# Attention block: pairing half of the second unit's maxima through key differences held in a slot of their own, and starting the half-run order at the third step

## The chip, the cores and the metric

One Trainium2 chip, and on it one core. The metric is the device time of one execution in microseconds (us); of several executions the median is given. A profile is one further execution, taken by the hardware profiler.

## What is computed

A transformer block on 2048 tokens of width 576, in float32: an adaLN modulation from a vector c, softmax attention with 32 heads of 18, and a gated feed-forward part of width 4608. The case is about the attention:

```python
q, k, v = split_heads(h @ wqkv)                  # h: layernorm(x) * (1 + ca) + sa
scores = einsum("bhqd,bhkd->bhqk", q, k) * 18 ** -0.5
p = softmax(scores)                              # over the 2048 keys
x = x + ga * (einsum("bhqk,bhkd->bhqd", p, v) @ wo)
x = x + gb * ((sigmoid(h2 @ w_gate) * (h2 @ w_up)) @ w_down)
```

The softmax subtracts the largest score of every row, so these maxima must be known before the exponentials of the row are taken.

## The kernel before

**Units and steps.** Attention runs over 32 units: a unit is two heads (h = 0, 1) and one half of the queries (1024). Unit u has 16 steps (kt = 0 to 15), one for each 128 keys; step number `step` is 16 u + kt. A step computes four score tiles s of 128 keys by 512 queries (PE, L1010), takes their exponentials p (ACT, L1014), and multiplies the values into them (PE, L584, `values()`). The values lag by two steps (`LAG = 2`).

**Maxima, run ahead.** The generator `maxima()` finds the row maxima of a unit long before its steps. Each call (a "turn") multiplies 128 queries by 512 keys into one PSUM bank (PE, L479) and takes the largest of every row (DVE, L485, `tensor_reduce`). A unit has 64 turns: 8 blocks `qt` of queries, by two heads, by four blocks `kc` of keys. Four turns go with a step. 88 turns have run before step 0 (the 64 of unit 0 and the blocks qt = 0, 1, 2 of unit 1), so the turns of step n are 88 + 4n to 91 + 4n; unit 1's blocks qt = 4 to 7 are the turns of steps 2 to 9, and unit 2 begins at step 10. After a unit, L497 takes the maximum over kc, and `spread()` (a PE transpose, L510, and four DMAs, L519) writes it as two more rows of the q tile, where L1010 subtracts it.

**Pairs.** From unit 2 on (`SINGLE = (0, 1)` are the two left out), head 0 treats the key blocks 0 and 1 as a pair. The product for kc = 0 uses the differences of the keys of block 0 and block 1 in place of the keys of block 0; ACT applies Relu to it into the tile `over` (L488), and one DVE instruction (L490, `tensor_tensor_reduce`) adds the product of kc = 1 and takes the maximum, since max(a, b) = max(a - b, 0) + b. So of eight turns six are reduced by L485, one by L490 and one goes to ACT. Cell kc = 1 of the result is then not written, and a memset (L464, POOL) fills it with a low number. The differences are made during the projections (`key_differences`, POOL, L325 to L330), are written to the DRAM tile `kd` behind the keys, and come to the chip as columns 2048 to 2559 of a unit's key tile. The key tiles of units 0 and 1 (`t0`, `t1`) have 2048 columns and hold none.

**Two orders.** The instructions of PE and ACT are issued in the order in which the text writes them (`manual_schedule`). A pair of steps (even kt, odd kt) has one of two orders, written as letters: m a maxima turn, t a score tile with its exponential, v the values of one step, a and b its two halves, w, s, c, k side work. The plain order is "vtmmttmvtm", "ktmwttmctmm"; the order with half runs is "vmmtmmtsactt", "wmcmbkttmtmt". `state["halved"]` selects the second one; its condition has `step >= 10`, the step at which the pairs begin. It also sets the order of the eight turns (`MAXIMA_H`).

**Queues and space.** The order of DVE, POOL and SP (the queue that issues most DMAs) is set by a planner. An engine runs its instructions in order, so one that waits holds back those behind it. Between the projections and attention, `right.close()` frees the projection's pools on the right side: `hT` (the operand), `wpool` (weights) and `stage` (the tiles `pl`, from which L310 stores q and k to DRAM). In their space stand the pools `opool`, `big` and `slots`; `slots` has the key tiles k0, k1, k2 (units 2, 3, 4 and so on), whose rows of ones are set by a POOL memset (L425) ahead of the loads of `load_heads` (L447, L451), and two tiles w0 and w1 for background work. The first user of w0 is `load_mod` at step 16 in the text, a load of 288 KB (L101); with it go two loads of 1152 KB into `big` (L100). They are for `weigh`, a POOL chain (L114, L117), which `modulate` uses at step 34.

Of the kernel before, what the change touches and what calls it, by code (L numbers as in the profile page):

```python
# [15 lines left out]
F32 = mybir.dt.float32  # L16
F32R = mybir.dt.float32r
# [6 lines left out]
P = 128  # L24
S = 2048
# [3 lines left out]
DH = 18  # L29
VW = DH + 1  # L30
NT = S // P
NCH = S // 512
# [3 lines left out]
LOWEST = -3.4e38  # L36
# [10 lines left out]
LAG = 2  # L47

MAXIMA = ((1, 0), (0, 0), (1, 1), (0, 2), (1, 2), (0, 3), (0, 1), (1, 3))
SINGLE = (0, 1)  # L50
# [11 lines left out]
def tile_block(ctx, tc, x_in, wqkv, wo, w_gate, w_up, w_down, c_in, w_mod, out):  # L62
    nc = tc.nc
# [25 lines left out]
    def bank():  # L89

        turns["bank"] += 1
        return ps[turns["bank"] % 7].tile([P, 512], F32, name=f"s{turns['bank'] % 7}")
# [171 lines left out]
    kd = dram.tile([2, D, S + 512], F32R, name="kd")  # L264
# [165 lines left out]
    def heads(u):  # L430
        return qsets[u % 3], ksets[u if u < 2 else 2 + (u - 2) % 3]

    def load_heads(u):


        qs, ks = heads(u)
        half, p = divmod(u, H // 2)
        n = S if u < 2 else S + 512
        own = slice(half * HW, (half + 1) * HW)
        for h in range(2):  # L440
            rows = slice((2 * p + h) * DH, (2 * p + h + 1) * DH)
            two, one = (slice(64 * h + a, 64 * h + b) for a, b in ((0, 2 * DH), (2 * DH, 3 * DH)))
            nc.sync.dma_start(
                qs[two, :].bitcast(F32), qd[:, rows, own].rearrange("l f n -> f l n").bitcast(F32)
            )
            nc.sync.dma_start(qs[one, :].bitcast(F32), qd[0, rows, own].bitcast(F32))
            nc.sync.dma_start(  # L447
                ks[two, 0:n].bitcast(F32),
                kd[0, rows, 0:n].unsqueeze(1).to_broadcast([DH, 2, n]).bitcast(F32),
            )  # L450
            nc.sync.dma_start(ks[one, 0:n].bitcast(F32), kd[1, rows, 0:n].bitcast(F32))  # L451
# [3 lines left out]
    def maxima():  # L455


        n = HW // P
        last = None
        for u in range(UNITS):  # L460
            qs, ks = heads(u)
            mx = mxs[u % 2]
            if u not in SINGLE and u - 2 in SINGLE:
                nc.gpsimd.memset(mx[:, 0:n, 1], LOWEST)  # L464
            for i in range(8 * n):
                if last is not None and i == (9 if u == 1 else 8):
                    if u == 1:
                        for _ in spread(*last):
                            pass
                    else:  # L470
                        state["spread"] = last
                qt = i // 8
                pairs = u not in SINGLE
                h, kc = (MAXIMA_H if state.get("halved") else MAXIMA)[i % 8]
                rows = slice(64 * h, 64 * h + 3 * DH)
                paired = pairs and h == 0 and kc < 2
                at = NCH if paired and kc == 0 else kc
                sp = bank()
                nc.tensor.matmul(  # L479
                    sp, qs[rows, qt * P : (qt + 1) * P],  # L480
                    ks[rows, at * 512 : (at + 1) * 512], start=True, stop=True,
                )
                to = mx[:, h * n + qt, kc : kc + 1]
                if not paired:
                    nc.vector.tensor_reduce(to, sp, axis=AX.X, op=ALU.max)  # L485
                elif kc == 0:
                    over = small.tile([P, 512], F32, name="over", bufs=1)
                    nc.scalar.activation(over, sp, AF.Relu)  # L488
                else:
                    nc.vector.tensor_tensor_reduce(  # L490
                        out=over, in0=sp, in1=over, scale=1.0, scalar=LOWEST,
                        op0=ALU.add, op1=ALU.max, accum_out=mx[:, h * n + qt, 0:1],
                    )
                if i < 8 * n - 1:
                    yield
            nm = small.tile([P, 2, n], F32, name="nm")
            nc.vector.tensor_reduce(  # L497
                nm.rearrange("p h t -> p (h t)"), mx, axis=AX.X, op=ALU.max, negate=True
            )
            last = (qs, nm)  # L500
            yield
        for _ in range(8):
            yield
        state["spread"] = last

    def spread(qs, nm):

        n = HW // P
        tp = bank()[0 : 2 * n, 0:P]
        nc.tensor.transpose(tp, nm.rearrange("p h t -> p (h t)"), ident)  # L510
        yield
        mrows = small.tile([32 + 2 * n, P], F32R, name="mrows", bufs=1)
        parts = [mrows[32 * l : 32 * l + 2 * n] for l in range(2)]
        nc.scalar.copy(parts[0], tp)
        nc.vector.tensor_sub(parts[1], tp, parts[0].bitcast(F32))
        for h in range(2):
            for l, part in enumerate(parts):
                to = 64 * h + 3 * DH + l
                nc.sync.dma_start(  # L519
                    qs[to : to + 1, :].rearrange("l (t q) -> l t q", q=P).bitcast(F32),  # L520
                    part[n * h : n * (h + 1), :].bitcast(F32),
                )

    todo = maxima()
    state = {}

# [10 lines left out]
    with tc.tile_pool(name="wv1", bufs=1) as wvp:  # L537
# [3 lines left out]
        for i, parts in enumerate(tiles):  # L541
# [5 lines left out]
            for g in range(2):  # L547
                pl = project_qk([(wt, 2 * g), (wt, 2 * g + 1)], run if i else None)
                col, n = parts[-1]
# [11 lines left out]
    slots = ctx.enter_context(tc.tile_pool(name="slots", bufs=1, side="right"))  # L561
# [7 lines left out]
    bgs = ExitStack()  # L569
    bgp = bgs.enter_context(tc.tile_pool(name="bgp", bufs=1))  # L570
    load_heads(2)

    pending = []

# [390 lines left out]
    for u in range(UNITS):  # L965
        half, p = divmod(u, H // 2)
        qs, ks = heads(u)
# [4 lines left out]
        for kt in range(NT):  # L972
            step = u * NT + kt
            turns["to"] = 64 + 4 * LEAD + 4 * (step + 1)
            kcols = slice(kt * P, (kt + 1) * P)
            if kt % 2 == 0:
                heavy = state.get("next") == "g"
                hold = heavy and (kt == 2 or kt == 12 and u < UNITS - 1)
                state["halved"] = step >= 10 and (hold or not heavy)
            halved = state["halved"]  # L980
            sides = iter(SIDES_H if halved else SIDES)
            probs = [None] * 4
# [1 line left out]
            for does in order[kt % 2]:  # L984
# [21 lines left out]
                else:  # L1006
                    c, h = next(sides)
                    sT = bank()
                    rows = slice(64 * h, 64 * h + 3 * DH + 2)
# [6 lines left out]
            if u in (1, 3):  # L1016
                if kt == 0:
                    a = big.tile([P, 8, 640], F32, name="big")
                    a = a.rearrange("p a b -> p (a b)")[:, 0 : 8 * D].rearrange("p (t c) -> p t c", t=4)
                    b = slots.tile([P, 2560], F32, name="w0")[:, 0 : 2 * D]  # L1020
# [519 lines left out]
    for n, (hf, b, k) in enumerate(seq):  # L1540
# [6 lines left out]
        at = n % 7  # L1547
# [196 lines left out]
```

## Time and profile before

| what | value |
|---|---|
| time, median of 3 runs (lowest to highest) | 2807.12 us (2804.7 to 2808.96) |
| the profiled execution | 2804.28 us |
| its span, first to last instruction | 2802.5 us |
| PE busy | 2766.7 us, 99% |
| DVE busy | 2299.2 us, 82% |
| ACT busy | 1606.0 us, 57% |
| POOL busy | 818.1 us, 29% |
| DMA traffic | 462.60 MB, mean 165 GB/s |
| granted TensorE clock | 1.000 |

A busy share is an average over stages that differ. The attention begins at about 236 us of the span; what a change there is worth is read from that stretch of the trace. In rows of the timeline the first number is the start in us, the second the time from the first to the end of the last instruction of the row, and the bracket at the end is the engine's idle time before it with what ended it. In rows of the windows the columns are the stretch, its length, the busy time and (number) of PE, PEld, DVE, ACT and POOL, the granted clock, the DMA engines' share and GB/s.

### The profile page before, as it was taken

Reading aid. Unit: us, or ns where it says so; the run is one execution under the profiler, and the core shown is the slowest. Engines: PE = TensorE matmul, PEld = TensorE weight load, DVE = VectorE, ACT = ScalarE, POOL = GpSimd, SP = SyncE. Lnnn points to the kernel's source line nnn. Section 1 sums busy time; section 2 is a strip of 40 time slices with the busy share of each in tenths; the row PEclk is TensorE's granted clock in tenths of the full one; section 3 lists DMA queues with packets and bytes.
Section 4 is the critical chain, followed back from the end, with each engine's and each line's share of the span. In section 5 each row is a group of like instructions: output and inputs, shape, how many; then the busy total and the mean of one; then the engine's idle time right before and its main releaser. Section 6 shows DMA issues by size and latency. Waiting matters only on the chain.

```text
span 2802.5 us, 50859 instructions
## 1 busy us (share of the span) xinstructions
PE 2766.7 (99%) x18637; PEld 1832.7 (65%) x18637; DVE 2299.2 (82%) x4370; ACT 1606.0 (57%) x3051; POOL 818.1 (29%) x1077
## 2 busy tenths in 40 slices
PE   7999999999999999999999999999999999999999
PEld 5975444444444444444443888888888888888888
DVE  7278999999998888999883788888898677777777
ACT  3216999999999778999888322333333222222221
POOL 3125208887843111563103222222221100000000
PEclk9999999999999999999999999999999999999999
DMA  5344215444432120222126766667767966666663
GB/s 173 126 148 148 75 59 172 164 171 161 172 135 80 36 58 24 98 106 66 48 68 216 269 217 228 233 216 266 279 249 275 356 200 196 203 195 201 200 196 120
DMA packets 170778, 462.60 MB, mean 165 GB/s; under 512 B 21212, under 2 KB 88032, under 8 KB 160416
## 3 DMA queue, kind: packets, MB, share of 16 engines
q1 hardware_dynamic: 150064, 360.72, 38.5%
q0 software_dynamic: 20464, 98.62, 10.0%
q8 instruction: 147, 2.41, 0.4%
q14 instruction: 103, 0.84, 0.1%
HBM read 281.92 MB, written 176.82 MB: 164 GB/s over the span
## 4 chain that ended last, share of the span: by engine, by line
PE 94%; DVE 3%; DMA 1%; ACT 1%; issue 1%; SPq 0%; POOL 0%; ACTq 0%; DVEq 0%; POOLq 0%
PE x L1151 27%; PE o L584 19%; PE s L1010 12%; PE s L479 11%; PE d L1301 8%; PE d L1233 6%; PE s L298 4%; PE s L731 2%; PE s L349 2%; DVE mx L485 1%; PE s L611 1%; ACT p L1014 1%; DMA wm<-in_w_mod_dram 0%; PE d L1480 0%; DVE w L1141 0%
## 5 line engine op out<-in xcount | busy, mean ns | idle before, releaser
L1014 ACT ACTIVATE p<-s 128x512 f32<-128x512 f32 x2048 | 1078.3, 622 | 99.2 <-PE s L1010 86.0
L485 DVE TENSOR_REDUCE mx<-s 128x1 f32<-128x512 f32 x1568 | 994.9, 684 | 111.4 <-PE s L479 97.3
L584 PE MATMUL o<-p,vaug 128*32 128x256 f32 (+1 forms) x5848 | 592.4, 477 | 3.0 <-ACT p L1014 2.5
L1010 PE MATMUL s<-q,k 56*128 56x512 f32 x1920 | 516.7, 449 | 0.0
L479 PE MATMUL s<-k,q 54*128 54x512 f32 x1920 | 501.2, 427 | 2.6 <-DVE t L701 1.7
L479 PEld LDWEIGHTS s<-k,q 54*128 54x128 f32 x1920 | 275.7, 185 | 232.1 <-DVE mx L490 161.0
L1010 PEld LDWEIGHTS s<-q,k 56*128 56x128 f32 x1920 | 246.9, 184 | 242.4 <-issue 112.8
L1151 PE MATMUL x<-k,w 128*128 128x512 f32 x1512 | 368.7, 391 | 0.0
L1151 PEld LDWEIGHTS x<-k,w 128*128 128x128 f32 x1512 | 277.0, 188 | 53.2 <-issue 1.7
L1301 PE MATMUL d<-wd,hh 128*128 128x288 f32 x1248 | 249.9, 295 | 2.4 <-DVE Oa L1305 2.4
L584 PEld LDWEIGHTS o<-p,vaug 128*32 128x32 f32 x5848 | 115.3, 108 | 209.4 <-issue 130.7
L1151 PE MATMUL x<-big,w 128*128 128x512 f32 x1008 | 244.7, 391 | 1.4 <-DVE u L1645 0.7
L1151 PE MATMUL x<-w,w 128*128 128x512 f32 x1008 | 245.1, 391 | 0.0
L1151 PEld LDWEIGHTS x<-big,w 128*128 128x128 f32 x1008 | 185.2, 188 | 37.4 <-DVE u L1645 1.1
L1151 PEld LDWEIGHTS x<-w,w 128*128 128x128 f32 x1008 | 184.3, 188 | 34.4
L1301 PEld LDWEIGHTS d<-wd,hh 128*128 128x128 f32 x1248 | 202.1, 188 | 6.3 <-DVE Oa L1305 3.1
L1301 PE MATMUL d<-wd,hl 128*128 128x288 f32 x624 | 184.3, 295 | 0.0
L1305 DVE TENSOR_TENSOR Oa<-Oa,d 128x288 f32<-128x288 f32 x312 | 136.5, 453 | 54.6 <-PE d L1301 50.5
L490 DVE CUSTOM_DVE_ANT_0 over<-s,over 128x512 f32<-128x512 f32 x240 | 164.7, 686 | 0.8 <-ACT p L1014 0.3
L488 ACT ACTIVATE over<-s 128x512 f32<-128x512 f32 x240 | 150.3, 626 | 7.5 <-PE s L479 7.3
L1160 ACT ACTIVATE sg<-x 128x512 f32<-128x512 f32 x36 | 21.6, 599 | 207.4 <-PE x L1151 207.4
L1132 ACT CAST w<-S 128x768 fp32r<-128x768 f32 x71 | 59.3, 836 | 137.2 <-POOL S L1105 135.4
(274 smaller groups left out, 3894.2 us busy)
## 6 DMA issues: line engine op xcount, KB each, us to landing
ws<-w SPq DMA_DIRECT2D x126, 640.0 KB
w<-ws SPq DMA_DIRECT2D x126, 640.0 KB
wd<-wds SPq DMA_DIRECT2D x19, 1152.0 KB
k<-kd SPq DMA_DIRECT2D x60, 360.0 KB
wds<-w POOLq DMA_DIRECT2D x18, 1152.0 KB, 4.9
wtd<-t POOLq DMA_DIRECT2D x32, 576.0 KB, 4.7
wt<-wtd SPq DMA_DIRECT2D x64, 288.0 KB
wd<-wds SPq DMA_DIRECT2D x52, 288.0 KB
```

The costliest lines, as they stand in the source:

```text
L298: nc.tensor.matmul(acc, w, hT[:, t, cols], start=n == 0, stop=n == len(ts_) - 1)
L479: nc.tensor.matmul(sp, qs[rows, qt * P : (qt + 1) * P], ks[rows, at * 512 : (at + 1) * 512], start=True, stop=True,)
L485: nc.vector.tensor_reduce(to, sp, axis=AX.X, op=ALU.max)
L488: nc.scalar.activation(over, sp, AF.Relu)
L490: nc.vector.tensor_tensor_reduce(out=over, in0=sp, in1=over, scale=1.0, scalar=LOWEST, op0=ALU.add, op1=ALU.max, accum_out=mx[:, h * n + q ...
L584: nc.tensor.matmul(acc[32 * j : 32 * j + 32, cols], vaug[:, kt, (2 * p + h) * VW : (2 * p + h) * VW + 32], probs[2 * c + h][:, cols], star ...
L1010: nc.tensor.matmul(sT, ks[rows, kcols], qs[rows, c * 512 : (c + 1) * 512], start=True, stop=True)
L1014: state["exp"] = nc.scalar.activation(pr, sT, AF.Exp, scale=SCALE)
L1151: nc.tensor.matmul(acc[v], w[:, v, a, :], X[s][:, b, :], start=first and n == 0, stop=n == 6, skip_group_check=not first,)
L1233: nc.tensor.matmul(acc, a[:, rows], w[:, k, :], start=n == 0, stop=n == 2)
L1301: nc.tensor.matmul(acc[:, :HALF], a[:, f, rows], w[:, f, cols], start=n == 0, stop=n == 5)
L1305: nc.vector.tensor_add(Oa[:, t, cols], Oa[:, t, cols], acc[:, :HALF])
```

## The change

Unit 1's blocks qt = 4 to 7 are paired too. Their differences come from a new tile, `state["differences"]`: the first 512 columns of w0, loaded by four DMAs on SP right after `load_heads(2)`; both heads are loaded, in the row layout of a key tile. POOL sets the cells kc = 1 of these blocks low. The order with half runs is allowed from step 2 (`LAG`) in place of step 10.

```diff
@@ maxima()
             if u not in SINGLE and u - 2 in SINGLE:
                 nc.gpsimd.memset(mx[:, 0:n, 1], LOWEST)
+            elif u == 1:
+                nc.gpsimd.memset(mx[:, n // 2 : n, 1], LOWEST)
...
-                pairs = u not in SINGLE
+                pairs = u not in SINGLE or u == 1 and 2 * qt >= n
                 h, kc = (MAXIMA_H if state.get("halved") else MAXIMA)[i % 8]
                 rows = slice(64 * h, 64 * h + 3 * DH)
                 paired = pairs and h == 0 and kc < 2
-                at = NCH if paired and kc == 0 else kc
+                keys = ks[rows, kc * 512 : (kc + 1) * 512]
+                if paired and kc == 0:
+                    keys = ks[rows, S : S + 512] if u > 1 else state["differences"][rows]
                 sp = bank()
                 nc.tensor.matmul(
                     sp, qs[rows, qt * P : (qt + 1) * P],
-                    ks[rows, at * 512 : (at + 1) * 512], start=True, stop=True,
+                    keys, start=True, stop=True,
                 )
@@ after load_heads(2)
+    kx = state["differences"] = slots.tile([P, 2560], F32R, name="w0")[:, 0:512]
+    for h in range(2):
+        rows = slice((2 + h) * DH, (3 + h) * DH)
+        two, one = (slice(64 * h + a, 64 * h + b) for a, b in ((0, 2 * DH), (2 * DH, 3 * DH)))
+        nc.sync.dma_start(
+            kx[two].bitcast(F32),
+            kd[0, rows, S : S + 512].unsqueeze(1).to_broadcast([DH, 2, 512]).bitcast(F32),
+        )
+        nc.sync.dma_start(kx[one].bitcast(F32), kd[1, rows, S : S + 512].bitcast(F32))
@@ the steps of attention
-                state["halved"] = step >= 10 and (hold or not heavy)
+                state["halved"] = step >= LAG and (hold or not heavy)
```

## The prediction

> **What bounds the kernel now.** First the page, for the whole span.
>
> ```profile
> span 2802.5 us, 50859 instructions
> PE 2766.7 (99%) x18637; PEld 1832.7 (65%) x18637; DVE 2299.2 (82%) x4370; ACT 1606.0 (57%) x3051; POOL 818.1 (29%) x1077
> PE 94%; DVE 3%; DMA 1%; ACT 1%; issue 1%; SPq 0%; POOL 0%; ACTq 0%; DVEq 0%; POOLq 0%
> L485 DVE TENSOR_REDUCE mx<-s 128x1 f32<-128x512 f32 x1568 | 994.9, 684 | 111.4 <-PE s L479 97.3
> L490 DVE CUSTOM_DVE_ANT_0 over<-s,over 128x512 f32<-128x512 f32 x240 | 164.7, 686 | 0.8 <-ACT p L1014 0.3
> L488 ACT ACTIVATE over<-s 128x512 f32<-128x512 f32 x240 | 150.3, 626 | 7.5 <-PE s L479 7.3
> ```
>
> PE sets the end almost alone: whatever makes PE wait anywhere is paid in full, because nothing later has slack to give it back. The change concerns eight steps of 512, so next comes the timeline of PE, to find them, and then the windows between the found times. Step 2's values begin at 240.44, step 10's at 260.58:
>
> ```profile
> 240.44 1.06 PE L584 MATMUL o<-p,vaug 128*32 128x512 f32 x8
> 241.44 0.73 PE L479 MATMUL s<-t,q 54*128 54x512 f32 x2
> 260.58 1.07 PE L584 MATMUL o<-p,vaug 128*32 128x512 f32 x8
> 261.58 0.73 PE L479 MATMUL s<-k,q 54*128 54x512 f32 x3
> 238.08 15.85 DVE L485 TENSOR_REDUCE mx<-s 128x1 f32<-128x512 f32 x26
> ```
> ```profile
> 240.44:245.42 4.98, 4.98 (x34) 2.10 (x32) 4.98 (x10) 4.00 (x9) 2.37 (x4) 1.00 1.00 349
> 245.42:250.47 5.05, 5.01 (x33) 1.91 (x32) 5.05 (x9) 4.13 (x10) 4.94 (x3) 1.00 0.59 169
> 250.47:255.53 5.06, 5.01 (x34) 1.91 (x33) 4.99 (x10) 4.14 (x10) 4.90 (x4) 1.00 0.59 192
> 255.53:260.58 5.05, 5.00 (x33) 1.90 (x32) 4.96 (x9) 4.12 (x10) 4.91 (x3) 1.00 0.53 168
> 260.58:265.20 4.62, 4.62 (x41) 1.88 (x40) 4.59 (x9) 3.85 (x9) 4.62 (x5) 1.00 0.10 30
> 270.13:274.76 4.63, 4.63 (x41) 1.89 (x40) 4.43 (x10) 4.49 (x10) 4.63 (x5) 1.00 0.01 3
> ```
>
> Each row is a pair of steps. In the first four (plain order, no pairs of keys) DVE, the third number after the length, is busy throughout: 26 reductions in a row took 15.85 us, 0.61 each, and eight of them are 4.9 of the 5.05 us. In the last two (half runs, with pairs) PE is full and DVE has some room. So steps 2 to 9 are bound by DVE, at 4.98 + 5.05 + 5.06 + 5.05 = 20.14 us, and the steps that follow by PE, at about 4.63.
>
> **The change, part by part.**
>
> *Pairing and order, steps 2 to 9 (taken together).* Four blocks, head 0: eight L485 (684 ns) leave and four L490 (686 ns) and four L488 on ACT (626 ns) come. That is one L485 fewer in each pair of steps. With the half-run order a pair of steps is then what the rows from 260.58 on show, 4.63 us. Alone this gives 20.14 - 4 x 4.63 = 1.6 us. ACT has the room: its 4.12 of 5.05 becomes 4.5 of 4.63. L479's product keeps its shape and costs the same. The new memset is 128x4 on POOL; the row of its kind, below, is 0.11 us behind 2.6 us of idle time, and POOL's idle time hides it. Between all (1.6) and nothing (0) I take 1.6, since the rows at 260.58 and after are the same instructions.
>
> *The four loads into w0.* This is where I expect the cost, so I read SP's timeline, its waits, and POOL.
>
> ```profile
> 236.40 0.38 SPq L100 DMA_DIRECT2D big<-in_w_mod_dram  x1
> 238.19 0.36 SPq L310 DMA_DIRECT2D qd<-pl  x1
> 238.60 0.67 SPq L100 DMA_DIRECT2D big<-in_w_mod_dram  x1
> 244.98 0.56 SPq L101 DMA_DIRECT2D w<-in_w_mod_dram  x1
> 248.27 0.81 SPq L447 DMA_DIRECT2D k<-kd  x1
> ```
> ```profile
> SPq L101 <- DMA qd<-pl: 5.5, 1, 5.5
> SPq L447 <- POOL k L425: 5.4, 4, 2.7
> ```
> ```profile
> 207.88 0.11 POOL L464 MEMSET mx<- 128x8 f32 x1 [2.60 <-DVE nm L497]
> 243.05 2.90 POOL L114 TENSOR_SCALAR big<-big,sc 128x576 f32<-128x576 f32 x4 [21.42 <-DMA big<-in_w_mod_dram]
> ```
>
> L101 is the first writer of w0 before the change. It waited 5.5 us, not for w0's own bytes but for the last store of the projections' `pl` tile (L310, issued 238.19): `slots` stands in the space of `stage`, and its first use waits until that pool is empty. In the changed kernel w0's first writers are the four new loads, so they inherit this wait. The planner has both `big` loads in SP's queue ahead of that point, since `big` needs only `hT`; so the store lands late, between two transfers of 1152 KB (the first, issued at 236.40, let POOL start only at 243.05). The new loads therefore start at 244.98 at the earliest.
>
> When do they land? Issue of the first is some 0.8 us (L447), so the second, which head 0's product needs too, is issued at about 245.8.
>
> ```profile
> 247.00:247.50 0.50, 0.50 (x8) 0.16 (x8) 0.50 (x2) 0.49 (x1) 0.50 (x1) 1.00 1.01 295
> 247.50:248.00 0.50, 0.50 (x8) 0.00 (x0) 0.50 (x2) 0.50 (x3) 0.50 (x1) 1.00 0.60 101
> 249.00:249.50 0.50, 0.50 (x5) 0.16 (x1) 0.50 (x2) 0.50 (x2) 0.50 (x1) 1.00 0.00 0
> 249.50:250.00 0.50, 0.46 (x3) 0.25 (x2) 0.50 (x2) 0.50 (x3) 0.50 (x1) 1.00 1.00 164
> kd<-kd_p POOLq DMA_DIRECT2D x1, 512.0 KB, 3.7
> ```
>
> The lower bound: the k load issued at 248.27 moves its first bytes in the window from 249.50, 1.2 us later; 245.8 + 1.2 = 247.0. The upper: the nearest row with a landing is POOL's store, 3.7 us for 512 KB; 245.8 + 3.7 = 249.5. The loads are small (36 and 18 rows of 2 KB), but the DMA engines are full with `big` until 247.5. I take T = 248.5. The Trainium skill, "DMA: Bandwidth & Descriptors", section "Anatomy of one DMA", gives about 2.0 us of fixed cost to a transfer, mostly completion; by that T would be about 247.8, an estimate inside these bounds, and no run here shows a small load of SP by itself.
>
> Who waits? In step 2 the order is v, m, m: the values (240.44 to 241.44), turn 96 on ordinary keys, and turn 97, the first product of differences, at about 241.6. PE is in order, and its order is fixed by the text, so all of PE stands behind turn 97 until T; DVE and ACT run dry after it. After T the rest of this pair takes 4.63 - 1.0 - 0.15 = 3.5 us, and three pairs more 13.9, so step 10's values begin at T + 17.4. Before it was 260.58. The net effect is T - 243.2: with T = 248.5 a loss of **5.3 us** (3.8 to 6.3), the gain of 1.6 being in it already.
>
> *The clock after the wait.* PE would stand still for 241.6 to 248.5, about 7 us; the idle times that PE has in this trace are far shorter, such as the 1.90 us below, and the mean granted clock is 1.000. The end of the run shows the other side.
>
> ```profile
> 38.38 0.53 PE L349 MATMUL s<-wv_h,hT 128*128 128x288 f32 x2 [1.90 <-DVE pl L305]
> 2799.00:2800.00 1.00, 0.36 (x3) 0.13 (x1) 0.51 (x2) 0.00 (x0) 0.00 (x0) 1.00 0.84 311
> 2801.00:2802.00 1.00, 0.00 (x0) 0.00 (x0) 0.00 (x0) 0.00 (x0) 0.00 (x0) 0.81 0.15 52
> 2802.00:2802.50 0.50, 0.00 (x0) 0.00 (x0) 0.00 (x0) 0.00 (x0) 0.00 (x0) 0.50 0.00 0
> 23.04 4.11 PE L215 MATMUL s<-ident,x 128*128 128x128 f32 x20 [0.74 <-DVE x L204]
> L215 PE MATMUL s<-ident,x 128*128 128x128 f32 x17 | 3.8, 417 | 0.7 <-DVE x L204 0.7
> L215 PE MATMUL s<-ident,x 128*128 128x128 f32 x10 | 1.7, 300 | 2.0 <-DVE x L204 2.0
> ```
>
> After the last matmul, at 2799.4, the clock goes from 1.00 to 0.50 within about 2.3 us (0.81 is the mean of that microsecond). So a standstill of 7 us would halve it. How long until it is back? At the start of the kernel the same transpose takes 417 ns up to 26.6 us and 300 ns after that (the last two rows are the windows 20 to 26.6 and 26.6 to 45), and the change comes inside a dense run that began at 23.04: 3.5 us of dense work. The bounds are 0 (as after the 1.90 us) and the whole time from the first matmul at 10.9 to 26.6, 15.7 us. At half the clock a PE-bound stretch loses half of its time: 0 to 7.9 us; I take half of 3.5, **1.8 us**. The Trainium skill has a rule for this, "TensorE: Matmul & The Clock Gate", section "What's actually happening": an idle window of about 3.4 us halves the clock, and a busy one of that length restores it; by that the term would be 1.7 us, an estimate. The trace agrees in size at both ends.
>
> *What is moved behind.* L101 (288 KB into w0) must now wait until the last product of differences has been issued, in step 8, some 14 us after T. POOL comes to that tile late:
>
> ```profile
> 270.91 1.47 POOL L114 TENSOR_SCALAR w<-w,sc 64x576 f32<-64x576 f32 x2
> 268.52 2.75 SPq L519 DMA_DIRECT2D q<-mrows  x4
> ```
>
> With L101 issued at about 263 and landed some 4 us later, POOL's row at 270.91 hides it; `modulate` at step 34 comes 45 us on. Behind L101 on SP stand the loads of k1 and the rows of maxima (L519), due later as well. Cost 0; if the planner put L101 ahead of k0's loads, these would wait, which is rival D's price.
>
> *Sum.* 5.3 + 1.8 = 7.1 us. The profiled execution (2804.28 us, 1.8 more than its span) would become 2811.4. The median of the runs stands 2.8 above it, so for the median 2807.1 + 7.1 = **2814.2 us**.
>
> **The rivals.**
>
> *B, a shorter wait or no loss of clock.* The wait of L101 speaks for some wait in every case; the sums without the clock term, or with T near 247, are +3.8 to +5.3: 2811 to 2812.4.
>
> *C, not slower: the differences are there in time.* If SP's queue has the new loads ahead of the `big` loads, the store of 238.19 meets idle DMA engines, the loads are issued near 240 and land about 242. The point that decides is T = 241.6; then PE never waits and the gain of 1.6 stays: 2805.5. For it: the new loads stand earlier in the text than `load_mod`. Against it: `big` is free at 236.3 and SP has nothing else to do, while the loads are not ready until the store has landed. Up to T = 243.2 the change costs nothing.
>
> *D, a longer wait.* If the loads come behind k0's four (issued from 248.27, held by the memset L425), they are issued near 252 and land near 256: 256 - 243.2 + 1.8 = 14.6, so 2822. Against it: they wait for no memset.
>
> *E, the order does not pay.* If the pairs of steps stay at 5.04 us, the 1.6 is missing: +8.7, 2815.8. The rows from 260.58 on speak against it.
>
> **How the numbers follow.** Chances: the sum above 0.60, B 0.15, C 0.13, D 0.08, E 0.04. A change under 0.2% (5.6 us) can't be told from none by a measurement of this kernel. Faster than that needs more than C gives: 0.04. Within it are C, most of B and the lower end of my case (T at 247): 0.26. Slower: the rest of my case, D and E: 0.70. The likeliest case's own range is 2811 (T = 247, some loss of clock) to 2818 (T = 249.5 and twice the clock term). The range for 8 in 10 takes in C and leaves out D: 2805 to 2819.
>
> **What would show it.** Right: PE idle from about 241.6 to 248 or 249 ahead of an L479, ended by a DMA into w; the new loads on SP at about 245, behind both L100; PEclk below 1.00 for some microseconds after; pairs of steps of 4.6 us from there to step 10; L101 after 260. From step 16 on the two traces run in parallel. Wrong: loads issued before 241, or a second wait of PE for k0.

## The result, and the profile after

| kernel | median (lowest to highest), us | ratio to before, 95% interval |
|---|---|---|
| before, in the same comparison | 2804.83 (2804.27 to 2808.96) | |
| the change | 2823.72 (2822.58 to 2825.07) | 1.0065 [1.0054, 1.0076] |

The change makes the kernel slower by 18.9 us, where 7.1 us were forecast. The sign was right; the size was not, and the time lies near that of rival D, outside the range that was forecast. The profiled execution took 2825.07 us, its span 2823.3. In the rows of after the line numbers have moved: the product of the maxima is L483 (was L479), the reduction L489 (L485), Relu L492 (L488), the pair's instruction L494 (L490), the values L597 (L584), the score tile L1023 (L1010). The new loads are L580 (two, to twice 18 rows each) and L584 (two, 18 rows each).

The page of after: the span, the shares of the chain that ended last, and three groups of instructions.

```profile
span 2823.3 us, 50950 instructions
PE 92%; DVE 4%; DMA 2%; ACT 1%; issue 1%; POOL 0%; SPq 0%; DVEq 0%; ACTq 0%; POOLq 0%
L489 DVE TENSOR_REDUCE mx<-s 128x1 f32<-128x512 f32 x1560 | 989.5, 683 | 129.4 <-PE s L483 103.2
L494 DVE CUSTOM_DVE_ANT_0 over<-s,over 128x512 f32<-128x512 f32 x244 | 167.2, 685 | 1.5 <-PE s L1023 1.0
L492 ACT ACTIVATE over<-s 128x512 f32<-128x512 f32 x244 | 152.7, 626 | 25.1 <-PE s L483 24.9
```

The instructions came out as counted: 1568 - 1560 = 8 reductions less, four pairs and four Relu more, at unchanged durations. What has grown is idle time that ends with PE's product (ACT's 7.3 us before such products became 24.9). So the cost is a wait of PE; its timeline says where.

```profile
239.63 1.07 PE L597 MATMUL o<-p,vaug 128*32 128x512 f32 x8
240.62 0.50 PE L483 MATMUL s<-t,q 54*128 54x512 f32 x1
257.29 0.76 PE L483 MATMUL s<-w,q 54*128 54x512 f32 x1 [16.16 <-DMA w<-kd]
278.10 1.06 PE L597 MATMUL o<-p,vaug 128*32 128x512 f32 x8
```

PE does turn 96 and then stands for 16.16 us behind turn 97, for the load of the differences. From the values of step 2 (239.63) to those of step 10 (278.10) the stretch now takes 38.47 us; before it took 20.14. That is +18.33 us, nearly the whole of the 18.9. The next view is the timeline of SP's queue in after (start, time, line, what is loaded):

```profile
235.59 0.38 SPq L100 DMA_DIRECT2D big<-in_w_mod_dram  x1
237.38 0.36 SPq L310 DMA_DIRECT2D qd<-pl  x1
237.79 0.46 SPq L100 DMA_DIRECT2D big<-in_w_mod_dram  x1
244.16 0.82 SPq L580 DMA_DIRECT2D w<-kd  x1
247.24 0.78 SPq L447 DMA_DIRECT2D k<-kd  x1
...
250.33 0.48 SPq L451 DMA_DIRECT2D k<-kd  x1
250.86 0.30 SPq L584 DMA_DIRECT2D w<-kd  x1
...
274.97 0.54 SPq L101 DMA_DIRECT2D w<-in_w_mod_dram  x1
```

The first new load stands where the prediction put it (244.16; 244.98 less the 0.8 us that everything before step 2 runs earlier in this execution). The second, L584 at 250.86, does not: four loads of k0 (two L447, two L451) stand between. Head 0's product needs both. Why these four took until 250.8 is in the chain of waits of after, in the stretch 238 to 280 (start, length, on what):

```profile
237.38 6.11 DMA qd<-pl
243.48 0.72 POOL big L114
...
244.99 2.22 POOL k L425
...
247.27 2.23 POOL k L425
249.52 0.76 SPq L447
...
250.33 0.48 SPq L451
...
250.86 6.34 DMA w<-kd
...
257.29 0.80 PE s L483 x2
```

Read upwards from the last line: PE's product waited for a load that took 6.34 us to land; that load waited for the issues of k0's loads ahead of it; these waited for two memsets of POOL of 2.2 us each (k0's rows of ones); and the memsets were held until 244.99, first by the late store of `pl` (6.11 us, between the two loads into `big`; e7 below moves these away), then by L114 on POOL. The stretch in windows, the wait first and then the four pairs of steps:

```profile
241.11:257.29 16.18, 0.01 (x2) 0.03 (x1) 1.10 (x3) 0.00 (x0) 14.94 (x10) 0.60 0.62 204
257.29:263.58 6.29, 6.29 (x31) 2.56 (x32) 2.90 (x5) 3.35 (x7) 6.21 (x6) 0.50 0.57 173
263.58:268.72 5.14, 5.14 (x42) 1.92 (x40) 4.05 (x9) 4.24 (x9) 5.14 (x6) 0.89 0.07 20
268.72:273.41 4.69, 4.69 (x42) 1.92 (x40) 4.38 (x10) 4.52 (x10) 1.15 (x1) 1.00 0.00 0
273.41:278.10 4.69, 4.69 (x42) 1.93 (x41) 4.33 (x9) 4.51 (x10) 0.00 (x0) 1.00 0.39 90
```

Three things are to be seen: the wait; then 6.29 us at a clock of 0.50 for the rest of the first pair, and 5.14 at 0.89; and from 268.72 on pairs of 4.69 us with PE full, as forecast (4.6). After the stretch the two traces run in parallel: the exponentials of later steps are 17.3 to 17.9 us late all through attention, and about 18.2 in the feed-forward part. In the profiled execution the distance grows by another 2.3 us, to 20.5, between about 2180 and 2260 us, where PE waits for DVE; waits of 1 us and more in that part vary from one profile to the next and are not put down to the change.

### The profile page after: what moved, and what is told of

Same layout as the page of the kernel before. It is cut to its first block, busy times and chain, and to the rows that moved or that the text cites. A ratio compares the mean times of both kernels' runs of the same rounds, so it can differ in the third digit from the quotient of the medians.

```text
span 2823.3 us, 50950 instructions
## 1 busy us (share of the span) xinstructions
PE 2769.0 (98%) x18669; PEld 1832.9 (65%) x18669; DVE 2296.0 (81%) x4370; ACT 1608.2 (57%) x3055; POOL 819.1 (29%) x1078
## 4 chain that ended last, share of the span: by engine, by line
PE 92%; DVE 4%; DMA 2%; ACT 1%; issue 1%; POOL 0%; SPq 0%; DVEq 0%; ACTq 0%; POOLq 0%
PE x L1164 26%; PE o L597 19%; PE s L1023 12%; PE s L483 10%; PE d L1314 8%; PE d L1246 6%; PE s L298 4%; PE s L744 2%; PE s L349 2%; DVE mx L489 1%; PE s L624 1%; ACT p L1027 1%; DMA raw<-in_B_w_up_dram 0%; DVE w L1154 0%; DMA wm<-in_w_mod_dram 0%
## 5 line engine op out<-in xcount | busy, mean ns | idle before, releaser
L489 DVE TENSOR_REDUCE mx<-s 128x1 f32<-128x512 f32 x1560 | 989.5, 683 | 129.4 <-PE s L483 103.2
L597 PE MATMUL o<-p,vaug 128*32 128x256 f32 (+1 forms) x5880 | 594.6, 476 | 3.1 <-ACT p L1027 2.5
L1023 PE MATMUL s<-q,k 56*128 56x512 f32 x1920 | 516.9, 449 | 0.0
L483 PE MATMUL s<-k,q 54*128 54x512 f32 x1920 | 501.9, 427 | 2.6 <-DVE t L714 1.7
L483 PEld LDWEIGHTS s<-k,q 54*128 54x128 f32 x1920 | 275.8, 185 | 231.8 <-DVE mx L494 159.3
L1023 PEld LDWEIGHTS s<-q,k 56*128 56x128 f32 x1920 | 247.0, 184 | 242.8 <-issue 112.8
L597 PEld LDWEIGHTS o<-p,vaug 128*32 128x32 f32 x5880 | 116.1, 108 | 211.8 <-issue 131.9
L494 DVE CUSTOM_DVE_ANT_0 over<-s,over 128x512 f32<-128x512 f32 x244 | 167.2, 685 | 1.5 <-PE s L1023 1.0
L492 ACT ACTIVATE over<-s 128x512 f32<-128x512 f32 x244 | 152.7, 626 | 25.1 <-PE s L483 24.9
```

The costliest lines, as they stand in the source:

```text
L483: nc.tensor.matmul(sp, qs[rows, qt * P : (qt + 1) * P], keys, start=True, stop=True,)
L494: nc.vector.tensor_tensor_reduce(out=over, in0=sp, in1=over, scale=1.0, scalar=LOWEST, op0=ALU.add, op1=ALU.max, accum_out=mx[:, h * n + q ...
L597: nc.tensor.matmul(acc[32 * j : 32 * j + 32, cols], vaug[:, kt, (2 * p + h) * VW : (2 * p + h) * VW + 32], probs[2 * c + h][:, cols], star ...
L1023: nc.tensor.matmul(sT, ks[rows, kcols], qs[rows, c * 512 : (c + 1) * 512], start=True, stop=True)
```

## The experiments

Two theories stood after this. **A**: the place of the loads in SP's queue makes the wait (k0's loads and POOL's memsets between them), the halved clock adds to it, and pairing itself gains 1.6 us. **B**: the new stretch is slower for another reason, and the order and pairs don't pay, or the loads disturb by their traffic. The time of before beside these runs was 2805.06 us for e1, e2, e6 and e7, and 2805.17 for the others. The profiles were taken of one execution each, so a time in a stretch is that of one execution. "Stretch" is always from the values of step 2 to those of step 10: 20.14 before, 38.47 with the change.

### e1_loads_first: the four loads ahead of k0's

```diff
-    load_heads(2)
     kx = state["differences"] = ...
     (the four loads)
+    load_heads(2)
```

> The changed kernel with the four loads of the differences written ahead of load_heads(2) instead of behind it. 'The stretch' is the time from the values of step 2 to the values of step 10: 20.14 us before, 38.47 us after the change. Theory A (the loss is made by k0's four loads, which stand in SP's queue between the first and the second load of the differences): the second load is issued at about 245, PE goes on at about 247.5, the stretch is 25.3 us and 1.8 to 3.3 us more for the clock, 27 to 28.6; the time is some 10 us under that of the change, about 2813. Rival B (the empty pool and the crowd of transfers make it late wherever it stands): PE goes on at 252 or later, the stretch is 30 us or more, 2816 or more. Rival C (the half-run order with pairs is itself slow at this place): the stretch less PE's wait stays above 22 us.

Measured: 2814.99 us (2812.94 to 2816.45), ratio 1.0033 [1.0021, 1.0046]. The store of `pl` in the chain of waits, timelines of SP and PE, and a window, of this kernel:

```profile
236.75 6.60 DMA qd<-pl
243.40 0.82 SPq L579 DMA_DIRECT2D w<-kd  x1
244.27 0.48 SPq L583 DMA_DIRECT2D w<-kd  x1
246.55 0.77 SPq L447 DMA_DIRECT2D k<-kd  x1
247.10 0.76 PE L483 MATMUL s<-w,q 54*128 54x512 f32 x1 [6.60 <-DMA w<-kd]
247.10:253.40 6.30, 6.30 (x32) 2.56 (x32) 2.90 (x5) 3.35 (x7) 6.16 (x3) 0.50 0.52 165
```

This is the queue that the prediction had assumed, and the wait (6.60 us) is the one that it forecast (about 7). That the time, 2814.99, is near its 2814.2 is in part luck: that sum stood on 2807.1 for before, and against the 2805.06 beside this run the cost is 9.9 us, not 7.1. The stretch is 28.67 us, 8.5 more than before: of the 18.3 us that the change costs there, the place behind k0's loads makes 38.47 - 28.67 = 9.8. The first pair after the wait again takes 6.3 us at a clock of 0.50.

### e2_tile_oT: the differences in a tile that is free early

The differences go to a tile `oT` of the pool `epool`, which stands in no space of the projections.

```diff
-    kx = state["differences"] = slots.tile([P, 2560], F32R, name="w0")[:, 0:512]
+    kx = state["differences"] = epool.tile([P, 512], F32R, name="oT")
```

> The changed kernel with the differences in the tile oT of epool (first used otherwise at step 17), whose space is free before the projections end, in place of w0. Theories A and B: the loads land before step 2, PE does not wait, the clock stays full, the stretch is 4 x 4.63 = 18.5 us, 1.6 under before; the time is 2803, within 0.2% of before and some 20 us under the change. Rival C: the stretch stays at 20 us or more.

Measured: 2806.48 us (2801.45 to 2812.13), ratio 1.0003 [0.9994, 1.0011]. SP's timeline, and the first and last pair of the stretch in the windows:

```profile
225.53 0.83 SPq L580 DMA_DIRECT2D oT<-kd  x1
240.78:245.56 4.78, 4.78 (x42) 2.05 (x40) 4.78 (x9) 3.82 (x8) 2.29 (x4) 1.00 1.01 351
254.87:259.55 4.68, 4.68 (x43) 1.93 (x41) 4.30 (x9) 4.50 (x10) 4.57 (x3) 1.00 0.60 165
```

The loads are issued 10 to 15 us before the stretch, PE waits for none, and the stretch takes 259.55 - 240.78 = 18.77 us: the whole of the loss is gone, and 1.4 us of the 1.6 forecast are gained. So the wait for w0 and what hangs on it is the cause. The gain of 1.4 us lies below what these times can tell, and they don't show it.

### e7_first_paced: e1, and the loads into `big` moved away as well

```diff
-            nc.sync.dma_start(a[:, t : t + 2, :], w_mod[rows, cols]...)
+            load = nc.sync.dma_start(a[:, t : t + 2, :], w_mod[rows, cols]...)
+            if i:
+                paced(load)
```

The loads into `big` are issued only beside step 16's exponentials, so the store of `pl` meets DMA engines without them.

> As e1 (loads first), and the two loads into big and their follower wait for the exponentials of step 16, so that they do not run beside the last store of the projections. If the crowd of these two transfers is what makes the pool empty late (244.0), the store lands at about 240, the loads of the differences are issued at 240 to 241.5, PE goes on at about 243.5, and the stretch is 21.3 us without loss of clock: about 2806. If the place in the queue was all, the stretch is that of e1 (27 to 28.6 us).

Measured: 2809.48 us (2807.32 to 2814.94), ratio 1.0017 [1.0008, 1.0025]. The store of `pl` in the chain of waits, timelines of SP and PE, and windows:

```profile
236.67 2.89 DMA qd<-pl
239.69 0.82 SPq L581 DMA_DIRECT2D w<-kd  x1
242.76 0.47 PE L485 MATMUL s<-w,q 54*128 54x512 f32 x1 [2.35 <-DMA w<-kd]
238.92:248.54 9.62, 7.27 (x42) 2.59 (x40) 5.44 (x11) 4.21 (x9) 8.71 (x4) 0.73 0.35 117
248.54:253.95 5.41, 5.41 (x43) 1.92 (x41) 4.06 (x9) 4.25 (x9) 4.64 (x3) 0.85 0.58 178
```

The store takes 2.89 us in place of 6.60, so the inherited wait ends 3.7 us earlier (239.69 after 243.40 in e1), and PE waits 2.35 us. That is nearly rival C of the prediction, whose point of no cost, 243.2, is 241.7 in this execution (it runs 1.5 us ahead): T is 242.76, 1.1 us past it. The stretch, 24.41 us, is 4.3 us shorter than in e1, but it costs 4.3 us more than before all the same, since even this short wait is followed by half speed (the rows above, with a clock of 0.73 and 0.85, hold 6.83 us of it); 21.3 us had been expected of the stretch without that.

### e6_kept_busy and e8_whole_array: PE kept busy in place of waiting

Products whose result is overwritten stand ahead of turn 97, so that PE has work while it waits. In e6 they have the shape of a maxima turn (54 rows), in e8 they fill the array (128 by 128).

```diff
+                if u == 1 and qt == n // 2 and paired and kc == 0:
+                    for _ in range(62):        # e6
+                        nc.tensor.matmul(sp, qs[rows, qt * P : (qt + 1) * P], ks[rows, 0:512], start=True, stop=True)
+                    for _ in range(66):        # e8
+                        nc.tensor.matmul(sp, ks[:, 0:P], ks[:, 0:512], start=True, stop=True)
```

> The changed kernel with 62 products of the same operands' size put on PE ahead of the first product of differences, into the same bank, which that product then overwrites: about 14 us of work in place of the 16.2 us of waiting. The outputs stay the same. If the clock's fall during the wait costs what the trace suggests (3.3 us: 2.8 in the first pair of steps after the wait and 0.5 in the second), the granted clock stays 1.00, PE goes on at 257.3 as in the change, the stretch is 35.2 us and the time 3 us under the change, 2820.5. Rival: the slow pairs come from DVE and ACT starting empty; then the stretch stays at 38.5 us and the time at 2823.7.

Measured: 2823.78 us (2819.93 to 2832.88), ratio 1.006 [1.0046, 1.0074]. PE's timeline and two windows:

```profile
237.00:238.00 1.00, 1.00 (x5) 0.52 (x4) 1.00 (x3) 1.00 (x4) 0.00 (x0) 0.58 1.11 359
240.26 26.39 PE L485 MATMUL s<-t,q 54*128 54x512 f32 x61
250.00:251.00 1.00, 1.00 (x4) 0.80 (x3) 0.00 (x0) 0.00 (x0) 0.94 (x2) 0.50 0.46 123
```

Inconclusive for the question, although the median, 2823.78, is the one that the rival had named. In the profiled execution, the slowest of the five (2832.88), the clock fell before these products began (0.58 in the microsecond from 237) and stayed at 0.50 through 26.4 us of them, so they took twice their time and made PE later than the wait would have. It does show that PE can be busy throughout in the profile and the clock stay down. The other four executions were not like this one: their mean granted clock is 0.998 or 0.999 (0.992 in the profiled one), which leaves no room for the 37.55 us at half speed that the profiled one has here; their times, 2819.93 to 2824.21, lie across both forecasts. Hence the second one.

> As e6, but with 66 products of 128 rows by 128 columns in place of 62 of 54 rows, some 15 us of work at full clock in place of the wait; the outputs stay the same. In e6's profile the clock had fallen already at 237.2 and stayed at 0.50 through 26 us of products that filled less than half of the array's rows. If the whole array's work keeps the clock up, PE goes on at about 257, the pairs of steps after it take 3.5 and 4.63 us (after the change 6.3 and 5.1), the stretch is 35.2 us and the time 2820.5. Rival: the clock's fall has no part in it; then the first pair after the wait takes 6 us again at a granted clock of 1.00.

Measured: 2818.93 us (2818.11 to 2821.18), ratio 1.0053 [1.004, 1.0067], 4.8 us under the change. The mean granted clock of its five executions is 0.999 or 1.000, that of the change's 0.993 to 0.996. PE's timeline and windows:

```profile
240.58 15.25 PE L485 MATMUL s<-t 128*128 128x512 f32 x66
256.77 0.47 PE L486 MATMUL s<-w,q 54*128 54x512 f32 x1 [0.94 <-PE s L485]
239.16:260.35 21.19, 20.25 (x109) 14.37 (x107) 5.26 (x11) 3.74 (x8) 18.34 (x12) 1.00 0.63 208
260.35:265.03 4.68, 4.68 (x43) 1.93 (x41) 4.32 (x9) 4.51 (x10) 4.68 (x5) 1.00 0.39 118
```

PE reaches turn 97 at almost the same distance from step 2 as with the change (17.61 us against 17.66), but at a full clock, and the first two pairs run at full speed. (The 0.94 us in the bracket are put down to PE's own products, but the load, issued at 250.49 and as late as with the change, fits them as well.) The stretch is 35.24 us, 3.2 less than with the change. That is the clock's share; DVE and ACT start empty here too, so the rival of e6 is out. The other 1.6 of the 4.8 us lie outside the stretch and were not traced; the profiled execution of the change has 2.3 us of its own there.

### e3_order_only and e4_pairs_only: the two halves alone

e3 keeps only the half-run order from step 2; the four loads, the pairs of unit 1 and the memset are out. e4 keeps the pairs, with the tile of e2, and the order begins at step 10 as before.

```diff
-                pairs = u not in SINGLE or u == 1 and 2 * qt >= n              # e3
+                pairs = u not in SINGLE
-                state["halved"] = step >= LAG and (hold or not heavy)          # e4
+                state["halved"] = step >= 10 and (hold or not heavy)
```

> The half-run order from step 2, without the pairs in unit 1 and without their loads. If the gain of the stretch comes from the pairs (one DVE reduction fewer in each pair of steps), DVE bounds the four pairs of steps as before, at eight times 0.61 us or more: 4.9 to 5.05 us each, the stretch 19.7 to 20.2 us, the time that of before. Rival: the half-run order brings the gain by itself; then the stretch is 18.5 to 18.8 us.

> The pairs in unit 1, with the differences in the tile oT, and the order with half runs from step 10 only. If the pairs make the gain, the stretch is near e2's 18.8 us although the order is the plain one; if pairs and order are both needed, it stays between 19.5 and 20.1 us. The time is within 0.2% of before in both cases.

Measured: e3 2807.64 us (2804.34 to 2808.85), ratio 1.0007 [0.9998, 1.0017], stretch 20.66 us. e4 2809.49 us (2805.93 to 2815.3), ratio 1.0019 [1.0009, 1.0028], stretch 21.24 us. The first and the second pair of e3, then the first and the third of e4, in the windows (the pairs behind the first are alike in each), and three of e4's waits (in all, number, longest):

```profile
238.69:244.06 5.37, 5.26 (x42) 2.26 (x40) 5.37 (x10) 3.65 (x8) 2.96 (x5) 1.00 1.02 362
244.06:249.16 5.10, 5.10 (x41) 2.20 (x41) 4.88 (x9) 4.24 (x9) 4.99 (x3) 1.00 0.54 150
```
```profile
241.30:247.19 5.89, 5.07 (x35) 1.97 (x33) 4.27 (x9) 5.22 (x11) 3.61 (x5) 1.00 1.01 354
252.31:257.42 5.11, 5.11 (x33) 1.95 (x32) 4.39 (x9) 4.51 (x11) 5.00 (x3) 1.00 0.57 178
ACT p L1027 <- PE s L483: 3.3, 4, 1.4
PEld s L1023 <- DVE mx L489: 5.0, 6, 0.8
DVE w L134 <- DMA qd<-pl: 1.6, 1, 1.6
```

Both lie above what had been expected of them (at most 20.2 and 20.1 us). In both the first pair is the long one: behind it the pairs take 5.09 to 5.12 us, hardly more than the 5.05 of before. So neither half gains; both together do (18.77 in e2). With the order alone DVE stays near full (4.88 of 5.10). With the pairs alone it is no longer full (4.39 of 5.11), as the count of reductions says, but in the plain order the exponentials still wait for PE and the weight loads of the score tiles for banks that DVE frees (3.3 and 5.0 us in e4's stretch; before it was 3.7 and 6.7). Why these waits keep the pair at its old length stays open. The 1.1 us that e4 loses in the stretch are for the most part not due to the pairs: in its first pair (5.89 us, 4.98 before) DVE stands 1.6 us in a memset into a `w` tile (L134), which waits for the late store of `pl`, and PE then 0.82 us for DVE; before, that memset ran at 253.88, long after the store. What lengthens the first pair of e3 stays open. The profile of e4 also holds a fall of the clock at about 1082 us, 6.8 us long, far from the stretch, so the 4.3 us by which e4's time stands above before are not all due to the pairs on that account either.

### e5_loads_only: the loads and the place of w0 alone

The four loads into w0 stay where the change has them, and nothing reads them; the pairs and the order are those of before.

```diff
-                pairs = u not in SINGLE or u == 1 and 2 * qt >= n
+                pairs = u not in SINGLE
-                state["halved"] = step >= LAG and (hold or not heavy)
+                state["halved"] = step >= 10 and (hold or not heavy)
```

> The kernel before with the four loads of the differences into w0, in the place that the change gives them, and nothing that reads them. If the loss is PE's wait for these loads, the stretch stays at 20.1 us, the clock stays full and the time is that of before, although L101 and POOL's work on w0 come later. Rival: the loads hold up k0's loads or the background work; then PE waits at step 10 or later and the time is above 2810.

Measured: 2804.81 us (2799.7 to 2807.72), ratio 0.9999 [0.9989, 1.0008]. Windows:

```profile
239.59:259.73 20.14, 20.00 (x131) 7.85 (x129) 19.99 (x35) 16.40 (x33) 17.30 (x11) 1.00 0.62 202
```

The loads are issued where the change has them (the first at 244.25, the second at 250.87). The stretch is 20.14 us, exactly that of before. The traffic and the issues of the loads cost nothing; only that PE waits for them does.

## Why the prediction was right or wrong

The prediction's net effect was T - 243.2, with step 2's values at 240.44; for any execution that is T less the start of step 2's values less 2.76. The same sum for the four kernels in which PE meets a late load, with the start of turn 97 for T (us):

| kernel | T less step 2's values | sum without clock (less 2.76) | stretch less 20.14 | left for the clock |
|---|---|---|---|---|
| forecast | 8.06 | 5.3 | 7.1 | 1.8 |
| e7 | 3.84 | 1.1 | 4.3 | 3.2 |
| e1 | 8.10 | 5.3 | 8.5 | 3.2 |
| the change | 17.66 | 14.9 | 18.3 | 3.4 |
| e8, clock kept at 1.00 | 17.61 | 14.9 | 15.1 | 0.2 |

**Right: the bound, the pairs, the place of the wait.** Pairs of 4.69 us after the wait, DVE not full, PE behind turn 97 on a DMA into w. The sum without the clock is met to 0.2 us where the clock was kept (e8), and for T anywhere from 3.8 to 17.7 us behind step 2 it leaves the same 3.2 to 3.4 us. The gain of 1.6 us was 1.4 (e2). But it was treated as one lump, and e3 and e4 show that it belongs to the pairs and the order together only.

**Wrong, and the greater part: "so the second, which head 0's product needs too, is issued at about 245.8", and with it T = 248.5.** It was issued at 250.86 and landed at 257.20. Against the forecast T, set back by the 0.8 us of this execution (247.7), that is 9.6 us, which with 1.6 us of clock is the whole distance from 7.1 to 18.3. Two assumptions failed. One is that the four loads stay together in SP's queue: the planner put k0's loads, which the text writes earlier, behind the first of them. The prediction had this as rival D and argued against it that the new loads "wait for no memset"; that is true of the loads and beside the point, because on an in-order queue they wait for whatever the loads ahead of them wait for, and k0's wait for L425. The other is the landing, with 3.7 us from issue as the upper bound: behind k0's transfers it took 6.34. D's price, +14.6, lacked 2 us of landing (258.0 in the times of before, where D had 256) and 1.6 us of clock; that its 2822 is so near the measured 2823.72 is in part luck, since it stood on 2807.1 for before and the comparison has 2804.83. In e1, where the assumed queue came true, T is 8.10 us behind step 2's values, and the forecast had 8.06: the landing that it had priced was right for that queue (though the rows up to 247.5 that it read as `big` hold L101's 288 KB as well, which the changed kernel moves away).

**Mis-sized: the clock term, 1.8 us (0 to 7.9).** It is 3.2 to 3.4 us in each of three kernels, whose waits were 2.35, 6.60 and 16.16 us, and 0.2 where PE had whole-array work; that 0.2 is in the others too, since the pairs take 4.68 or 4.69 us in place of 4.63, so the clock's own part is about 3 us. The step that failed is the return, "3.5 us of dense work": PE ran at half speed for about 7 us after the wait (257.29 until 264.7 with the change, 247.10 until 254.0 in e1). The 3.5 us had been read at the start of the kernel, in other products (transposes on 128 rows); why the return takes longer in attention stays open. The Trainium skill, "TensorE: Matmul & The Clock Gate", section "What's actually happening", has the full clock come back after at least one busy window of about 3.4 us; the estimate of 1.7 us took just one, and these traces show twice that time to the return. That estimate and the one from the rows erred in the same way.

**Right: the rest at nothing.** L101 was issued at 274.97 and its work on POOL was late too, and the offset to before stays between 17.3 and 17.9 us through attention; the loads as such cost 0 (e5).

**What stood in the way of C.** Its mechanism, a store that meets idle DMA engines, is e7: the loads are issued at 239.69, as C had it ("near 240"), yet land too late by 2.35 us, and the clock then takes more than the wait. The change keeps its 1.4 us in the stretch where the differences lie in space that no store of the projections holds (e2).

## What to carry to other kernels

Here a load that was put into space just freed waited for the last user of that whole space, and on its in-order queue for every wait of the loads that the planner had put ahead of it. So look for what stands earlier in the text and becomes ready at the same time, and price that order as a case of its own rather than assume that loads written together stay together. Where PE is the bound, a wait of even 2 us can cost its length and some 3 us more, lost to half speed after it. And two edits that pay together may each gain nothing alone, so test them apart before calling one of them the gain; and look in the trace whether a loss in such a test is the edit's own (e4's was mostly a memset that waited for a store).

## What the runs showed of the hardware that was not expected

- **The cost of the clock hardly depends on the length of the wait.** 2.35 us and 16.16 us of standstill both left 3.2 to 3.4 us of loss. In the clock records of these ten profiles every fall and every return lies a whole number of 3.41 us behind the first entry of its record: the half speed after the wait lasts 6.83 us in e7 (beginning 0.6 us after PE went on), 10.24 in e1, 20.48 with the change.
- **The same short wait can leave the clock alone or halve it.** A wait of 1.9 us in the projections stands in every one of the profiles, and only in e6 did half speed begin in it; the wait of 2.02 us that follows it in all but e6 was followed by half speed in e1 alone (from 42.41, the wait's end being 42.30); a gap of some 0.9 us between 1077 and 1106 us stands in all, and half speed followed it in e2, e3 and e4 alone, for 3.41, 6.83 and 6.83 us. That it depends on where a wait falls between two such times is likely, but was not tested; a length that decides can't be read from these runs.
- **Busy is not always enough.** In one execution, 26.4 us of products that use 54 of the array's 128 rows, one after the other, ran with the granted clock at 0.50 throughout (e6), after a fall before them; in the other four the clock can't have stayed down like that. Products on 128 rows, begun at full clock, held it at 1.00 through 15 us (e8). The ordinary steps, whose score tiles and values are mixed with such products, recover. Whether e6's clock was held down by the shape was not tried by itself.
- **Where a small load stands in the queue changes its landing.** The second new load was on the chip less than 2.9 us after its issue in e1 (244.27, PE on at 247.10), and took 6.34 us behind k0's loads (360 and 180 KB each) with the change. The DMA engines were not full meanwhile (59.5% from 250 to 258), so how the loads ahead hold it back is not shown.
